# Attention and state space in one kernel: a smaller table base built on GpSimd, value sums dealt period by period, and a reordered tail

## The chip, the cores and the metric

The kernel runs on one core of a Trainium2 chip. The metric is the device time of one launch in microseconds; a figure quoted for a kernel is the median of its runs (at a granted clock of 0.995 to 1.0). The profile's span is some 1.8 us shorter than the device time of the same run (920.3 for 922.11), so spans are compared with spans and times with times.

## The reference, cut to what matters

Two layers read the same input x (2048 tokens, 1024 features, bf16), and a gate mixes them.

```python
g = sigmoid((x * gate_w).sum(-1, keepdims=True))
# a: state space, 1024 complex states, a scan over 2048 tokens
h_t = Lam_bar * h_{t-1} + (x @ B_bar.T)_t
a   = 2.0 * einsum("blp,dp->bld", h, Cmat).real + x * Dskip
# b: attention, 32 heads of 32 features
q, k, v = split(x @ wqkv)
b = softmax(q @ k.T * 32 ** -0.5) @ v   ... @ wo
return g * a + (1 - g) * b
```

The softmax has 32 x 2048 x 2048 = 134 million exps. They set the scale of everything that follows.

## The kernel before

The attention is cut into 512 **bursts**. A burst is 4 heads x 256 keys x 256 queries: 8 score matmuls fill two slots of PSUM, the memory that matmuls write to (two banks each), and ScalarE takes the exp of each slot (128x1024). A **half burst** is one of which VectorE computes half of the first exp by integer arithmetic; ScalarE then does 128x512 and 128x1024. `DVB` is the list of them.

```python
def exp(self, B, z, s):
    ...
    if z == 0 and B in DVB:
        self.dve_exp(B, s, p)          # ScalarE 128x512, VectorE the other 512 in four steps
    else:
        self.act(lambda e: e.activation(self.tile[p], ps[:, 2 * s:2 * s + 2, :], ACT.Exp, ...), [("S", s)], [("pt", p)], "exp")
```

From score to score of the next burst is one **period**. In it TensorE does the burst's 8 score matmuls, some **quarters** (a quarter is a fourth of an earlier burst's value sums: 4 matmuls of 128x33) and some **wide** matmuls (128x512) of whatever else the kernel needs: projections, the state-space products, the output product. (The value projection's are 128x128; four of them count as a wide one here.) The wide ones come in chains of 8 or 16 (a few of 7), all of them into the one PSUM bank 7, and after a chain VectorE has to copy that bank out before the next chain may start.

```python
for p in range(first, NBURST):
    second = self.burst(p)                    # 8 score matmuls, first exp
    head, tail = self.split_pv(p, ntail)      # this period's quarters: most ahead of, a few behind the wide ones
    self.pv(head)
    second()                                  # second exp
    quota = 3 if p in DVB else 5 if p + 1 in DVB and ... else MM_PER_PERIOD     # 4
    while used < quota:                       # wide matmuls; chains all go to bank 7
        ...
    self.pv(tail)
    ...
    ended.evac()                              # VectorE empties bank 7 after a chain's end
```

How many quarters a period takes is decided ahead, by a simple rule, in `plan`: five, or three in a half burst and in the period ahead of one (now and then one more).

```python
cap = 5
if p in DVB or p + 1 in DVB:
    cap = 3
```

The exps of a burst lie in a ring of tiles until their quarters have run, so quarters can't be put off for long.

## Time and profile before

| | before |
|---|---|
| device time, median of 6 runs | 921.74 us (921.26 to 922.04) |
| span of the profiled run | 920.3 us |
| TensorE / ScalarE / VectorE / GpSimd busy | 884.9 / 904.4 / 758.0 / 6.5 us |
| start to first exp | 9.8 us |
| first exp's start to last exp's end | 901.7 us |
| last exp's end to the span's end | 8.8 us |

Two engines are near 100%, and the question is which of them sets the end and how much is lost between. The prediction below shows the lines and reads them. The costliest groups of the page before: line, engine, operation, output and inputs, shapes, count, then busy time and mean ns, then idle time before them and what ended it. PE is TensorE, PEld its weight loads, ACT ScalarE, DVE VectorE, POOL GpSimd, SP the engine whose sequencer issues most DMAs; a q behind a name means the sequencer.

### The profile page before, as it was taken

To read this page: it belongs to the slowest core of one execution; us is meant where nothing else is said; L and a number is where in the kernel's file an instruction comes from. 1 tells how busy PE (TensorE), PEld (TensorE's weight loads), DVE (VectorE), ACT (ScalarE), POOL (GpSimd) and SP (SyncE) were. 2 spreads that over 40 slices of the span, in tenths; PEclk is the share of its full clock that TensorE was granted. 3 is DMA by queue.
4 is the path that set the end of the run, shared out by engine and by line. 5 is a ranking of instruction groups with operands and counts; after the bars stand their busy time and mean duration, and the time that the engine had idled before them with its cause. 6 is when DMAs were issued, how large, how long until landed. Compare 5 with 4: busy or idle time off the path is not lost.

```text
span 920.3 us, 33392 instructions
## 1 busy us (share of the span) xinstructions
PE 884.9 (96%) x14969; PEld 516.3 (56%) x15188; DVE 758.0 (82%) x1369; ACT 904.4 (98%) x1034; POOL 6.5 (1%) x31
## 2 busy tenths in 40 slices
PE   8999999999999999999999999999999999999996
PEld 4556655755575555565557555556655655555553
DVE  2799999999989889999889975669999866675665
ACT  6999999999999999999999999999999999999996
POOL 0000000000000000000000000000000000000000
PEclk9999999999999999999999999999999999999998
DMA  9546822213302324112142113123320212524312
GB/s 200 111 82 114 120 48 40 47 42 73 82 9 56 62 59 93 47 36 53 51 82 43 42 46 86 44 63 53 51 64 8 68 60 82 162 78 131 113 63 75
DMA packets 166436, 65.35 MB, mean 71 GB/s; under 512 B 146704, under 2 KB 154896, under 8 KB 166288
## 3 DMA queue, kind: packets, MB, share of 16 engines
q1 hardware_dynamic: 164128, 62.62, 30.6%
q8 instruction: 120, 1.97, 0.9%
q10 hardware_dynamic: 2160, 0.53, 0.3%
q14 instruction: 28, 0.23, 0.1%
HBM read 21.24 MB, written 12.58 MB: 37 GB/s over the span
## 4 chain that ended last, share of the span: by engine, by line
ACT 69%; PE 25%; DVE 2%; SPq 1%; issue 1%; DMA 1%; DVEq 0%
ACT f_pt L1693 59%; PE f_ps L1765 7%; PE f_ps L1677 5%; PE f_ps L1513 4%; PE f_ps L1485 4%; PE f_ps L1453 3%; ACT f_wb L1716 2%; ACT f_OT L1693 2%; ACT f_Et L1693 2%; ACT f_cT_re L1693 2%; ACT f_cT_im L1693 2%; PE f_ps L1473 1%; ACT f_ub L1716 1%; SPq L1080 1%; DMA f_xT<-in_A_x_dram 1%
## 5 line engine op out<-in xcount | busy, mean ns | idle before, releaser
L1693 ACT ACTIVATE f_pt<-f_ps 128x1024 bf16<-128x1024 f32 x848 | 801.8, 1141 | 1.2 <-PE f_ps L1677 1.0
L1765 PEld LDWEIGHTS f_ps<-f_V,f_pt 128*128 128x128 bf16 x6784 | 235.0, 96 | 136.5 <-issue 86.6
L1765 PE MATMUL f_ps<-f_V,f_pt 128*128 128x33 bf16 x6784 | 288.4, 178 | 0.3
L1677 PE MATMUL f_ps<-f_Q,f_K 32*128 32x256 bf16 x4096 | 217.9, 273 | 6.8 <-ACT f_cT_re L1693 1.0
L1677 PEld LDWEIGHTS f_ps<-f_Q,f_K 32*128 32x128 bf16 x4096 | 70.3, 92 | 122.6 <-ACT f_pt L1693 62.3
L1485 PE MATMUL f_ps<-f_xT,f_wb 128*128 128x512 bf16 x449 | 117.5, 377 | 7.2 <-issue 2.4
L1453 PE MATMUL f_ps<-f_xT,f_wb 128*128 128x512 bf16 x406 | 106.6, 378 | 5.0 <-issue 1.0
L1399 DVE TENSOR_TENSOR_SCAN f_ht<-f_pf,f_init,f_ut 128x512 bf16<-128x512 f32 x64 | 81.0, 1274 | 0.0
L1717 DVE TENSOR_SCALAR f_wb<-f_ps 128x512 f32<-128x512 f32 x77 | 52.8, 686 | 27.7 <-PE f_ps L1677 27.2
L1513 PE MATMUL f_ps<-f_cT_im,f_hp 128*128 128x512 bf16 x183 | 69.1, 378 | 3.0 <-DVE f_Ag L1522 0.5
L1540 PE MATMUL f_ps<-f_wb,f_OT 128*128 128x512 bf16 x219 | 58.0, 378 | 2.1 <-DVE f_xT L1546 0.2
L1473 PE MATMUL f_ps<-f_wb,f_xT 128*128 128x128 bf16 x896 | 59.1, 219 | 0.0
L1485 PEld LDWEIGHTS f_ps<-f_xT,f_wb 128*128 128x128 bf16 x512 | 40.2, 96 | 33.4 <-issue 1.2
L1513 PE MATMUL f_ps<-f_cT_re,f_hp 128*128 128x512 bf16 x153 | 57.8, 378 | 0.6
L1716 ACT ACTIVATE f_wb<-f_ps 128x512 bf16<-128x512 f32 x77 | 53.8, 699 | 0.0
L1724 DVE SCALAR_TENSOR_TENSOR f_wb<-f_Ag,f_wb 128x512 int16<-128x512 f32 x77 | 52.7, 684 | 0.7
L1723 DVE SCALAR_TENSOR_TENSOR f_Ag<-f_wb,f_Ag 128x512 f32<-128x512 uint16 x77 | 52.7, 685 | 0.6
L1722 DVE SCALAR_TENSOR_TENSOR f_Ag<-f_wb 128x512 f32<-128x512 uint16 x77 | 52.6, 683 | 0.1
L1453 PEld LDWEIGHTS f_ps<-f_xT,f_wb 128*128 128x128 bf16 x464 | 36.2, 96 | 28.7 <-issue 0.4
L1473 PEld LDWEIGHTS f_ps<-f_wb,f_xT 128*128 128x128 bf16 x896 | 50.5, 97 | 0.2
L1546 DVE SCALAR_TENSOR_TENSOR f_xT<-f_ps,f_gcol,f_hp 128x512 bf16<-128x512 f32 (+1 forms) x28 | 21.0, 751 | 26.6 <-PE f_ps L1540 26.6
L1391 DVE TENSOR_TENSOR f_tq<-f_ht,f_Et 128x1024 bf16<-128x1024 bf16 x64 | 42.5, 685 | 0.3
(143 smaller groups left out, 872.1 us busy)
## 6 DMA issues: line engine op xcount, KB each, us to landing
ag_scratch<-f_Ag SPq DMA_DIRECT2D x32, 256.0 KB, 2.0
f_hp<-ag_scratch SPq DMA_DIRECT2D x32, 256.0 KB, 2.8
f_wb<-in_B_wqkv_dram SPq DMA_DIRECT2D x21, 256.0 KB, 4.1
out_dram<-f_xT SPq DMA_DIRECT2D x16, 256.0 KB, 2.0
f_xa<-in_A_x_dram SPq DMA_DIRECT2D x32, 64.0 KB, 2.0
f_pf<-in_A_x_dram SPq DMA_DIRECT2D x32, 64.0 KB, 2.0
f_wb<-in_B_wo_dram SPq DMA_DIRECT2D x1, 1024.0 KB
f_OT<-f_On SPq DMA_TRANSPOSE x63, 2.3
```

The lines of the kernel that those rows point to most:

```text
L1399: ops.append((1.192, lambda ri=ri: dve(lambda e: e.tensor_tensor_scan(ht[:, ri, :], rr, ut[:, ri, :], self.init[:, ri, j:j + 1], ALU.mult, ...
L1453: mms.append((1, lambda e, f, l, a=a: e.matmul(ps[:, bank, :], w[:, g % 2, part, a, :], xT[:, a, 512 * ch:512 * (ch + 1)], start=f, stop=l ...
L1473: m = e.matmul(ps[:, bank, 128 * q:128 * (q + 1)], xT[:, a, 128 * kt:128 * (kt + 1)], w[:, g % 2, 2, a, :], start=(a == 0), stop=(a == 7))
L1485: mms.append((1, lambda e, f, l, a=a: e.matmul(ps[:, 7, :], bT[:, n % 2, ri, a, :], xT[:, a, 512 * ch:512 * (ch + 1)], start=f, stop=l), [ ...
L1513: mms.append((1, lambda e, f, l, j=j, ri=ri: e.matmul(ps[:, 7, :], hp(tq, ri, j), cT[ri][:, j, 512 * cb:512 * (cb + 1)], start=f, stop=l), ...
L1540: mms.append((1, lambda e, f, l, j=j: e.matmul(ps[:, 7, :], OT[:, j, 256 * qb + 128 * r:256 * qb + 128 * (r + 1)], wo[j][0][:, 512 * cb:51 ...
L1677: m = e.matmul(ps[:, 2 * sl[z] + h % 2, 256 * kl:256 * (kl + 1)], K[32 * h:32 * h + 32, g % 2, 128 * kt:128 * (kt + 1)], Q[32 * h:32 * h + ...
L1693: self.act(lambda e: e.activation(self.tile[p], ps[:, 2 * s:2 * s + 2, :], ACT.Exp, bias=OCTAVES * LN2, scale=LN2 / 128), [("S", s)], [("p ...
L1716: self.S.op("act", lambda e: e.activation(t[:, 0, :], ps[:, 2 * s, :], ACT.Exp, bias=OCTAVES * LN2, scale=LN2 / 128), reads=[("S", s)], wr ...
L1717: self.S.op("dve", lambda e: e.tensor_scalar(xi, ps[:, 2 * s + 1, :], BITS_0, BITS_MIN, ALU.add, ALU.max), reads=[("S", s)], writes=[("xi" ...
L1723: (0.603, lambda: self.dve(lambda e: e.scalar_tensor_tensor(xw, lo, CUBE_C, xw, ALU.add, ALU.mult), [I, W], [W], "exp_c")),
L1765: m = e.matmul(ps[:, 6, o:o + 33], self.tile[p][:, h2, 256 * kl + 128 * qt:256 * kl + 128 * (qt + 1)], V[:, g % 2, 2 * i + kl, h, :], star ...
```

## The change

The intent was to take work from ScalarE and VectorE and to even out TensorE's periods:

- The table of powers that the scan needs was built on VectorE from products of 512. Now GpSimd makes a base of 128 steps (six operations), and VectorE doubles it twice.
- From burst 72 on the quarters of a period are chosen as the kernel is built: as many as fit under the estimated end of ScalarE's exps, at most 7, never fewer than the tile ring forces (`least`).
- The lists `ORDER` (which chain comes when) and `DVB` (half bursts: 96 before, 102 after, none past burst 506) are new.
- The last burst's exps are split by query rows instead of heads, so that one row half can be normalized while the other is in ScalarE. The output is stored in four parts instead of two, and the long range check runs before the tail.
- The last four partial output products are prepared in two parts, and the second part is issued three times over (the result of the last counts).

The diff has 776 lines; this is its core, with cuts marked.

```diff
-DVB_RUNS = ((65, 65), (70, 70), ... (501, 501), (508, 508))
+DVB_RUNS = ((70, 70), (73, 73), ... (493, 497), (502, 506))
+PV_FREE = 72
+PV_MOST = 7
+PV_ROUND = 0.5
...
+    def pv_pick(self, p, dense, ta):
+        todo = self.pv_todo[self.pv_done // 32]
+        ready = sum(1 for t in todo if t[0] <= p)
+        least = self.pv_need[p] - self.pv_done
+        n = int((ta - self.T - QK_PE - dense * MM_PE - 0.1) / PV_PE + PV_ROUND)
+        n = max(min(n, PV_MOST), least, 1)
...
+        for n, (u, v) in enumerate(((0, 0), (1, 1), (0, 1), (1, 0))):
+            self.pool(lambda e, n=n, u=u, v=v: e.tensor_tensor(pr[n], hi[u], lo[v], ALU.mult), ...)
+            if n % 2:
+                self.pool(lambda e, ...: e.tensor_tensor(out, pr[n - 1], pr[n], ALU.add if r else ALU.subtract), ...)
...
+        if kind == "rest":
+            def again(e, f, l):
+                for _ in range(3):
+                    m = e.matmul(ps[:, 7, :], OT[:, 7, ...], wo[7][0][:, ...], start=True, stop=True)
+                return m
...
+        if B == NBURST - 1:
+            for t in range(2):
+                self.act(lambda e, t=t: e.activation(<row half t of all four heads>, ACT.Exp, ...), [("S", 1), ("S", 2)], ...)
```

## The prediction

> **What bounds the kernel now.** I read the page first: the busy line of the engines, the chain that ended last, and the top group.
>
> ```profile
> span 920.3 us, 33392 instructions
> ...
> PE 884.9 (96%) x14969; PEld 516.3 (56%) x15188; DVE 758.0 (82%) x1369; ACT 904.4 (98%) x1034; POOL 6.5 (1%) x31
> ...
> ACT 69%; PE 25%; DVE 2%; SPq 1%; issue 1%; DMA 1%; DVEq 0%
> ...
> L1693 ACT ACTIVATE f_pt<-f_ps 128x1024 bf16<-128x1024 f32 x848 | 801.8, 1141 | 1.2 <-PE f_ps L1677 1.0
> ```
>
> ScalarE (ACT) is busy 98% and holds 69% of the chain. It does nothing but softmax exps: 512 bursts of scores, two exps of 128x1024 each. In 96 bursts VectorE takes half of the first exp, so that ScalarE does 928 full exps (848+24+20+18+18 in the groups by shape) and 96 half ones (77+19). But PE is at 96%, so "busy" hides small losses. They show only in the distance from start to start. The second view is the timeline of ACT in the opening (start, length, engine, line, tile):
>
> ```profile
> 23.10 1.05 ACT L1693 ACTIVATE f_cT_re<-f_ps 128x1024 bf16<-128x1024 f32 x1
> 24.01 1.07 ACT L1693 ACTIVATE f_cT_im<-f_ps 128x1024 bf16<-128x1024 f32 x1
> 24.91 1.08 ACT L1693 ACTIVATE f_cT_re<-f_ps 128x1024 bf16<-128x1024 f32 x1
> ```
>
> The spans are 1.05 us or more and overlap; a new exp starts every 0.904 us (23.10, 24.01, 24.91). Taken over all starts in the trace, the least distance is 0.904 us after a full exp (its median too) and 0.477 us after a half one. So ScalarE's **floor** is 928 x 0.904 + 96 x 0.477 = 838.9 + 45.8 = 884.7 us. The first exp starts at 9.82, the last ends at 911.52: 901.7 us, so some 17 us are lost between exps. What stays is 9.8 us of opening and 8.8 us of tail.
>
> Third, where those 17 us go. Summing the distance over the floor, burst by burst: bursts 16 to 71 lose 2.7 us, 72 to 500 lose 13.2 us, 501 to 510 0.2 us; the rest is opening. Nearly every large loss comes before a burst's first exp and waits for its scores (PE, L1677). An example from the timeline of 644.7 to 649:
>
> ```profile
> 644.76 0.51 PE L1677 MATMUL f_ps<-f_Q,f_K 32*128 32x256 bf16 x8
> 645.20 0.47 PE L1765 MATMUL f_ps<-f_V,f_pt 128*128 128x33 bf16 x12
> 645.52 1.24 PE L1485 MATMUL f_ps<-f_xT,f_wb 128*128 128x512 bf16 x5
> 646.59 0.36 PE L1765 MATMUL f_ps<-f_V,f_pt 128*128 128x33 bf16 x8
> 646.88 0.40 PE L1677 MATMUL f_ps<-f_Q,f_K 32*128 32x256 bf16 x8
> ```
>
> One period: 8 score matmuls, 20 value-sum matmuls (5 quarters of 4), 5 wide ones. Scores come again after 2.12 us, while two full exps need 1.81 us. The kernel's own constants (scores 0.34, a quarter 0.101, a wide matmul 0.2157, 0.1 over) give 0.34+0.505+1.079+0.1 = 2.02 us here, and 1.91 for 6 quarters and 4 wide, where the trace has 1.905. I sorted the 429 periods from 72 to 500 by that formula. In 39 PE is over ScalarE's floor by more than 20 ns: **5.2 us** lost. In 35 it is not, yet over 60 ns are lost (**5.3 us**), mostly where a wide chain waits for VectorE to empty its bank. The others add 2.7 us of crumbs. In sum PE needs 690 us there by the formula and ScalarE 736: the work fits, it is badly dealt.
>
> Fourth, the end of the chain of waits, in order of time:
>
> ```profile
> 912.03 0.17 DVE f_rc L2060
> ...
> 912.23 0.37 DVE f_On L2063 x2
> ...
> 913.24 0.61 PE f_ps L2078 x2
> 913.84 0.11 PE f_ps L2081
> ...
> 914.05 0.68 DVE f_xT L2091
> 914.73 0.34 DVEq L2149
> 915.07 0.24 DVE f_xT L2091
> ```
>
> This serial tail follows the last exp (ends 911.52): reciprocal, normalize, transpose, output product, addition. The sequencer records add that the last store is issued at 915.39 to 915.72, and its sixteen parts land from 917.31 to 919.81; instruction-fetch packets of 8 and 16 KB run among them from 915.7 on. Then 0.45 us to the end.
>
> **What the Trainium skill says.** "ScalarE: Activation LUTs", on what ACT_TABLE_LOAD costs, gives 280 ns + 0.833 ns per element for an ACTIVATE with a pointer bias, 1133 ns at 1024, and an overlap of some 93 ns back to back. The lengths agree (1106 median), the overlap does not: starts are 904 ns apart, and I use that. "GPSIMD Engine Reference", 3.1, has a tensor_tensor of 2048 fp32 elements at 4497 ns, twice VectorE's; no run here has a large one yet (the largest in the trace is 128x8, 0.2 to 0.3 us). "Runtime: NRT & Kernel Launch", Instruction fetch mechanics, says a taken branch outside the current pages forces a fetch by DMA; the packets at the end of this trace agree.
>
> **The change part by part.**
> Exps: the two lists of bursts count 96 and 102. Six more halves move to VectorE: 6 x (0.904 - 0.477) = **-2.6 us** of ScalarE's floor. The last burst's exps by row halves keep their size.
>
> VectorE: six more exps cost 6 x 4 x 0.685 = 16.4 us. The tables cost 16 x 1.215 + 16 x 0.685 = 30.4 us before; after, by the costs written in the change, 8 x 2.35 = 18.8, so -11.6. The sine chain goes from 400 to 224 columns: 19 instructions at about 0.47 to 0.34, some -2.5. The 24 small copies at 0.161 go to GpSimd: -3.9. Sum -18: VectorE comes out level. GpSimd gets 6 operations of 1024 elements, an estimate from the skill's figure of 2.25 us each, 13.5 us in a row. They can start once the sine chain is done, which the new spare slots put near 26 us; ready near 40, just when the tables are wanted (the opening's 16 bursts end at 38.6). I count 0.
>
> Value sums dealt per period: from burst 72 on, a period takes as many quarters as fit under ScalarE's end, at most 7. With 5 wide matmuls it takes 3 instead of 5, with 4 it takes 5, with 3 it takes 7. The 39 overfull periods go, but rounding and the limits of the tile ring leave some: 5.2 to about 1, **-4.2 us**. Of the 5.3 us of late banks little: **-0.8 us**. Before burst 72 nothing.
>
> Tail: one query row half is finished while the other's exp runs, so one normalize (0.27) leaves the path, the flag product (0.11) goes behind, the reciprocal is cheaper. Against it, on VectorE the short check (0.8 us) and two additions (2 x 0.68) stay in a row after the last normalize. From the last exp's end E: value sums to E+0.42, reciprocal and normalize to 1.05, check to 1.85, additions to 3.25, last store issued by E+3.65, where it was E+4.2: -0.55. The stores are four of half the size, two queues are used, and the branches come after the last issue rather than before, so that fewer packets should stand behind fetches: another -1 of the 2.5 us between first and last landing. Together **-1.5 us**. The repeated product in the last four partial outputs adds 8 wide matmuls on PE, 1.7 us, where PE has 2.9 us spare over ten periods: 0.
>
> Sum: -2.6 - 5.0 - 1.5 = -9.1; 921.7 - 9.1 = **912.6 us**.
>
> **Rivals.**
> PE as the bound: it is 96% busy and a full period with 5 quarters and 4 wide ones takes 1.81 us by the formula, all that ScalarE gives. If shorter exps only turn into waits for scores, the -2.6 goes and half of the dealing: 917. For it: those balanced periods lose 35 ns on average already. Against: 46 us of slack over 429 periods.
> VectorE and GpSimd: if the base is late, VectorE stands in order before its table work, the bank is not emptied, and ScalarE stalls in the opening; likewise six more exps among slices where DVE already shows 9. For it: 13.5 us in a row on GpSimd is only an estimate. Worth +2 to +4: 915 to 917.
> The dealing works better than I grant: all overfull periods and half of the late banks vanish, crumbs halve: -4 more, 908.
> The end: fetches still hit the stores; then -0.5 for -1.5, 913.6.
>
> **Range and chances.** The middle is 912.6; rivals push up 1 to 5 and down 4. I take 907.5 to 917.5. Over 2% faster means below 903.3, that is 9.8 + 882.1 + a 7 us tail with almost no loss: 0.03. Slower by 2%: 0.01.
>
> **What would show it.** ScalarE's groups: 922 exps of 128x1024 and 102 of 128x512. The loss between exps at 11 to 13 us instead of 17; no period with 5 wide matmuls and 5 quarters past burst 72. On GpSimd six operations near 2.2 us ending by 41 us, and no long wait of VectorE for POOL. From the last exp's end to the span's end 7.3 us instead of 8.8. The prediction is wrong if periods with 4 wide matmuls lose more than before, or if VectorE waits for GpSimd.

## More of the kernel before

```profile
L1485 PE MATMUL f_ps<-f_xT,f_wb 128*128 128x512 bf16 x449 | 117.5, 377 | 7.2 <-issue 2.4
...
L1485 PEld LDWEIGHTS f_ps<-f_xT,f_wb 128*128 128x128 bf16 x512 | 40.2, 96 | 33.4 <-issue 1.2
```

Every matmul of this line loads its weights once. So 512 were run and the trace has the records of 449.

## The result, and the profile after

| | before | after |
|---|---|---|
| device time, median of 6 runs each | 921.74 us | 918.81 us (918.65 to 919.24) |
| ratio of fast runs, 95% interval | | 0.9969 (0.9956 to 0.9982) |

Ratios here are the mean time of one kernel's fast runs over that of the other's in the same rounds, so not quite the ratio of the medians. The change won 2.9 us where 9.1 were predicted, and 918.8 lies above the range of 907.5 to 917.5. The result is correct.

The page after, its busy line, its chain that ended last and the top groups of ScalarE:

```profile
span 916.8 us, 33709 instructions
...
PE 902.4 (98%) x15196; PEld 513.6 (56%) x15196; DVE 757.3 (83%) x1394; ACT 902.1 (98%) x1034; POOL 33.4 (4%) x63
...
PE 92%; DVE 3%; ACT 3%; DMA 1%; issue 0%; SPq 0%
...
L1781 ACT ACTIVATE f_pt<-f_ps 128x1024 bf16<-128x1024 f32 x840 | 800.5, 1156 | 1.2 <-PE f_ps L1758 0.6
```

VectorE is level, as foreseen. But the chain seems to have gone from ScalarE (69%) to TensorE (92%), and TensorE's busy time rose by 17.5 us, though the change adds only 1.7 us of matmuls. That is a trap. This time no record is missing:

```profile
L1517 PE MATMUL f_ps<-f_xT,f_wb 128*128 128x512 bf16 x512 | 131.1, 377 | 1.5 <-DVE f_ub L1523 0.4
...
L1517 PEld LDWEIGHTS f_ps<-f_xT,f_wb 128*128 128x128 bf16 x512 | 40.3, 96 | 34.2 <-issue 2.2
```

The changed kernel was run once more later (after_control below), and that trace again lacked 219 records. The same kernel then reads like this:

```profile
PE 882.0 (96%) x14977; PEld 513.5 (56%) x15196; DVE 757.4 (83%) x1394; ACT 902.3 (98%) x1034; POOL 33.4 (4%) x63
...
PE 75%; ACT 18%; DVE 3%; issue 2%; SPq 1%; DMA 1%
```

Seven of the twenty traces lack 217 to 219 records, the one of before among them. evac_less_before below, which has the matmuls of before and lacks no record, shows PE busy for 903.5 us and in 71% of the chain. So neither PE's busy time nor the chain's shares may be compared between a full trace and one with gaps. What is safe are the exps, of which each trace has all 1024, and LDWEIGHTS, which agree with the program in all traces.

From the exps' starts, the span falls into these stages (us; the third column is the repeat of after):

| stage | before | after | repeat |
|---|---|---|---|
| to the first exp | 9.82 | 9.77 | 9.66 |
| bursts 0 to 15 | 29.68 | 29.40 | 29.68 |
| bursts 16 to 71 | 103.06 | 103.08 | 103.07 |
| bursts 72 to 500 | 749.54 | 747.86 | 747.45 |
| bursts 501 to 510 | 17.39 | 17.42 | 17.42 |
| burst 511, to the last exp's end | 2.03 | 2.05 | 2.05 |
| tail | 8.79 | 7.26 | 7.26 |

Two stages moved: bursts 72 to 500 by -1.7 (-2.1 in the repeat), the tail by -1.5. (The profiled run of before, 922.11 us, is 0.4 over its median, so the stages differ by more in sum than the medians do.) In 72 to 500 the **floor** of ScalarE (0.904 us for each full exp, 0.477 for each half one, as in the prediction) fell from 736.3 to 733.4, by 3.0, since there are 7 more half bursts in that stage. But the loss over the floor rose from 13.2 to 14.5 us, where I had it fall by 5.0. Sorted by the kind of period (matmuls counted by their weight loads; rare kinds left out):

| periods of 72 to 500 | before: number, mean loss | after: number, mean loss |
|---|---|---|
| full, 5 quarters, 5 wide | 38, 127 ns | none |
| full, 4 quarters, 5 wide | none | 23, 109 ns |
| full, 3 quarters, 5 wide | 46, 44 ns | 57, 46 ns |
| full, 5 quarters, 4 wide | 139, 24 ns | 153, 9 ns |
| full, 6 quarters, 4 wide | 6, 71 ns | 5, 68 ns |
| all full bursts | 337, 11.4 us in sum | 330, 8.6 us in sum |
| half, 3 quarters, 3 wide | 81, 12 ns | 72, 45 ns |
| half, 4 quarters, 3 wide | none | 14, 73 ns |
| half, 5 quarters, 3 wide | none | 6, 203 ns |
| all half bursts | 92, 1.8 us in sum | 99, 5.9 us in sum |

The dealing helped in the full bursts (-2.8 us), most of all in those with four wide matmuls, and gave more than that back in the half ones (+4.1). The 5.9 us of the half bursts have two parts: 2.2 are lost after the 20 with four or five quarters; and of the 72 with three quarters, the 28 in whose period TensorE stands over 60 ns at a chain's start lose 2.7, the other 44 only 0.5. An example of each from the timeline of the kernel after (start, length, engine, line, tiles). The first is a half burst with five quarters (20 value matmuls, of which the cut lines leave 8 to see):

```profile
841.00 0.40 PE L1758 MATMUL f_ps<-f_Q,f_K 32*128 32x256 bf16 x8
...
841.32 0.37 PE L1853 MATMUL f_ps<-f_V,f_pt 128*128 128x33 bf16 x8
841.43 0.64 ACT L1804 ACTIVATE f_ub<-f_ps 128x512 bf16<-128x512 f32 x1
...
841.74 0.81 PE L1578 MATMUL f_ps<-f_wb,f_OT 128*128 128x512 bf16 x3
841.92 1.06 ACT L1781 ACTIVATE f_pt<-f_ps 128x1024 bf16<-128x1024 f32 x1
...
842.58 0.29 PE L1758 MATMUL f_ps<-f_Q,f_K 32*128 32x256 bf16 x4
```

From scores to scores TensorE takes 842.58 - 841.00 = 1.58 us without a gap, and ScalarE has 0.477 + 0.904 = 1.38 us of work: 0.2 us are lost. The second is a half burst in which a chain starts:

```profile
703.72 0.40 PE L1758 MATMUL f_ps<-f_Q,f_K 32*128 32x256 bf16 x8
703.83 0.69 DVE L1493 CAST f_K<-f_ps 128x512 bf16<-128x512 f32 x1 [0.20 <-PE f_ps L1485]
...
704.05 0.47 PE L1853 MATMUL f_ps<-f_V,f_pt 128*128 128x33 bf16 x12
...
704.66 0.83 PE L1505 MATMUL f_ps<-f_wb,f_xT 128*128 128x128 bf16 x12
```

VectorE empties bank 7 until 703.83 + 0.69 = 704.52. The three quarters, issued at some 25 ns a matmul, are through by 704.05 + 12 x 0.025 = 704.35. The next chain starts at 704.66: 0.3 us of TensorE are lost, and the period takes 1.70 us for a floor of 1.38.

GpSimd did what was foreseen, and VectorE found the base ready (the timeline of POOL; the first table operation of VectorE comes at 40.13):

```profile
26.24 3.82 POOL L1319 TENSOR_TENSOR f_hp<-f_rc 128x1024 f32<-128x1024 f32 x2 [23.33 <-DVE f_rc L1310]
...
36.36 2.36 POOL L1323 TENSOR_TENSOR f_OT<-f_hp 128x1024 f32<-128x1024 f32 x1
```

The tail after, from the chain of waits in order of time (start, length, what; the last exp ends at 909.58):

```profile
910.06 0.21 PE f_ps L2173 x8
...
910.51 0.37 DVE f_On L2181 x2
...
913.48 0.69 DVE f_xT L2203
```

### The profile page after: what moved, and what is told of

Same layout as the page of the kernel before. It is cut to its first block, busy times and chain, and to the rows that moved or that the text cites. A ratio compares the mean times of both kernels' runs of the same rounds, so it can differ in the third digit from the quotient of the medians.

```text
span 916.8 us, 33709 instructions
## 1 busy us (share of the span) xinstructions
PE 902.4 (98%) x15196; PEld 513.6 (56%) x15196; DVE 757.3 (83%) x1394; ACT 902.1 (98%) x1034; POOL 33.4 (4%) x63
## 4 chain that ended last, share of the span: by engine, by line
PE 92%; DVE 3%; ACT 3%; DMA 1%; issue 0%; SPq 0%
PE f_ps L1853 26%; PE f_ps L1758 18%; PE f_ps L1545 12%; PE f_ps L1517 12%; PE f_ps L1485 11%; PE f_ps L1578 6%; PE f_ps L1505 5%; ACT f_cT_re L1781 1%; DVE f_tq L1423 1%; ACT f_pt L1781 1%; DMA f_xT<-in_A_x_dram 1%; ACT f_cT_im L1781 1%; ACT f_Et L1781 1%; ACT f_OT L1781 1%; DVE f_ht L1431 1%
## 5 line engine op out<-in xcount | busy, mean ns | idle before, releaser
L1758 PE MATMUL f_ps<-f_Q,f_K 32*128 32x256 bf16 x4096 | 213.1, 273 | 2.6 <-ACT f_cT_re L1781 1.2
L1517 PE MATMUL f_ps<-f_xT,f_wb 128*128 128x512 bf16 x512 | 131.1, 377 | 1.5 <-DVE f_ub L1523 0.4
L1485 PE MATMUL f_ps<-f_xT,f_wb 128*128 128x512 bf16 x464 | 119.0, 378 | 0.3 <-DVE f_Q L1490 0.2
L1805 DVE TENSOR_SCALAR f_wb<-f_ps 128x512 f32<-128x512 f32 x83 | 56.8, 685 | 27.4 <-PE f_ps L1758 26.5
L1545 PE MATMUL f_ps<-f_cT_re,f_hp 128*128 128x512 bf16 x192 | 72.6, 378 | 0.9 <-DVE f_Ag L1554 0.8
L1578 PE MATMUL f_ps<-f_wb,f_OT 128*128 128x512 bf16 x248 | 63.9, 378 | 0.2
L1804 ACT ACTIVATE f_wb<-f_ps 128x512 bf16<-128x512 f32 x83 | 60.8, 732 | 0.6 <-PE f_ps L1758 0.6
L1812 DVE SCALAR_TENSOR_TENSOR f_wb<-f_Ag,f_wb 128x512 int16<-128x512 f32 x83 | 56.7, 683 | 0.6
L1811 DVE SCALAR_TENSOR_TENSOR f_Ag<-f_wb,f_Ag 128x512 f32<-128x512 uint16 x83 | 56.7, 683 | 0.5
L1810 DVE SCALAR_TENSOR_TENSOR f_Ag<-f_wb 128x512 f32<-128x512 uint16 x83 | 56.6, 682 | 0.3
L1523 DVE CAST f_ub<-f_ps 128x512 bf16<-128x512 f32 x48 | 33.1, 690 | 14.8 <-PE f_ps L1517 14.1
```

Of the source, the lines that this page charges most:

```text
L1485: mms.append((1, lambda e, f, l, a=a: e.matmul(ps[:, bank, :], w[:, g % 2, part, a, :], xT[:, a, 512 * ch:512 * (ch + 1)], start=f, stop=l ...
L1517: mms.append((1, lambda e, f, l, a=a: e.matmul(ps[:, 7, :], bT[:, n % 2, ri, a, :], xT[:, a, 512 * ch:512 * (ch + 1)], start=f, stop=l), [ ...
L1545: mms.append((1, lambda e, f, l, j=j, ri=ri: e.matmul(ps[:, 7, :], hp(tq, ri, j), cT[ri][:, j, 512 * cb:512 * (cb + 1)], start=f, stop=l), ...
L1578: mms.append((1, lambda e, f, l, j=j: e.matmul(ps[:, 7, :], OT[:, j, 256 * qb + 128 * r:256 * qb + 128 * (r + 1)], wo[j][0][:, 512 * cb:51 ...
L1758: m = e.matmul(ps[:, 2 * sl[z] + h % 2, 256 * kl:256 * (kl + 1)], K[32 * h:32 * h + 32, g % 2, 128 * kt:128 * (kt + 1)], Q[32 * h:32 * h + ...
L1804: self.S.op("act", lambda e: e.activation(t[:, 0, :], ps[:, 2 * s, :], ACT.Exp, bias=OCTAVES * LN2, scale=LN2 / 128), reads=[("S", s)], wr ...
```

## The experiments

Runs of the kernel before on the same chip (medians 921.64, 921.28, 921.58, 922.15, 921.58). **My theory** after the traces: TensorE and ScalarE need nearly the same time in almost every period, neither has slack to lend from one period to the next, and the new dealing pushes quarters into half bursts and away from the boundaries between chains. **Rival A**: ScalarE alone is the bound and the loss is latency. **Rival B**: TensorE alone is the bound, as the chain's 92% suggest. **Rival C**: VectorE is too full to empty the bank in time.

### Which engine is the bound: 42 us less of TensorE, 29 us less of ScalarE, both

pe_less cuts one matmul of eight in each chain from 512 to 32 columns, act_less the full exps from burst 100 on from 1024 to 976 elements. pe_less is wrong; act_less leaves some exps stale and yet stays in tolerance. My texts put pe_less at 30 us. The traces have 218 shortened matmuls, after which the next one starts 25 ns later and not 215, or the next scores 110 and not 311: about 42 us. For act_less, 727 exps (in after) that may follow 0.04 us sooner are the 29 us expected.

```diff
-  mms.append((1, lambda ...: e.matmul(ps[:, bank, :], w[...], xT[:, a, 512 * ch:512 * (ch + 1)], ...)))
+  n = 32 if a == 3 else 512          # the same in the u, c and output chains
+  mms.append((1, lambda ...: e.matmul(ps[:, bank, 0:n], w[...], xT[:, a, 512 * ch:512 * ch + n], ...)))
```

```diff
-  e.activation(self.tile[p], ps[:, 2 * s:2 * s + 2, :], ACT.Exp, ...)
+  n = 488 if B >= 100 else 512
+  e.activation(self.tile[p][:, :, 0:n], ps[:, 2 * s:2 * s + 2, 0:n], ACT.Exp, ...)
```

> The kernel before, with one wide matmul in each chain of eight (two in each of sixteen) cut from 512 to 32 columns: about 200 matmuls, some 30 us of TensorE work less, everything else as it was; the result is wrong on purpose. Theory 1 (TensorE's work is as long as ScalarE's, its seeming slack of 46 us was lost matmul records): the 13 us lost between the exps fall to about 4, so 912 us. Theory 2 (the prediction's own: ScalarE alone is the bound, TensorE only badly dealt): the overfull periods go, 915 to 917 us. Theory 3 (banks emptied late by VectorE): 919 or more.

> The kernel before, with every full exp from burst 100 on cut from 1024 to 976 elements: some 730 exps by 0.04 us, 29 us of ScalarE work less; the result is wrong on purpose. Theory 1: TensorE takes over at once, no more than 5 us are won, 917 us or more. Theory 2: with 46 us of slack on TensorE most of it is won, 895 to 902 us. Theory 3: most of it too, the late banks stay, 897 to 905 us.

> The kernel after with the same cut of TensorE work. Theory 1: from 918.8 to some 909 us, a larger fall than before, as ScalarE's floor is 2.6 us lower and the six halves become visible. Theory 2: 916 us. Theory 3: 917 us or more.

> The kernel after with the same cut of ScalarE work. Theory 1: 914 us or more. Theory 2: 892 to 900 us. Theory 3: 894 to 902 us.

> The kernel after with both cuts of the last runs: TensorE by some 30 us and ScalarE by 29. Each alone won only 4. Theory 1b (the two are equally long period by period, and what one spares in one period cannot be kept for the next): the two cuts together win more than the sum of both, 15 us or more: 904 us or less. Theory 3 (late banks rule): the sum at most, 911 us or more. The result is wrong on purpose.

| run | time, us | ratio to before (95%) | against its own base |
|---|---|---|---|
| pe_less_before | 918.98 | 0.9975 (0.9959 to 0.9992) | -2.7 |
| act_less_before | 917.94 | 0.9960 (0.9943 to 0.9977) | -3.7 |
| pe_less_after | 914.60 | 0.9924 (0.9907 to 0.9941) | -4.2 |
| act_less_after | 914.93 | 0.9928 (0.9911 to 0.9944) | -3.9 |
| both_less_after | 893.62 | 0.9699 (0.9682 to 0.9715) | -25.2 |

(The base is the kernel before, 921.64, or the first figure of after, 918.81.) In pe_less_after the pauses among the eight score matmuls of a burst, summed over bursts 72 to 500, grew from 50 to 88 us: TensorE waits there for about as long as it no longer works. The chains that ended last say who is left as the bound; pe_less_after:

```profile
ACT 90%; PE 8%; SPq 1%; DMA 1%; DVE 0%; issue 0%
```

and act_less_after:

```profile
PE 90%; DVE 4%; ACT 3%; DMA 1%; issue 1%; SPq 0%; DVEq 0%
```

**What follows.** Either cut alone wins 3 to 4 us, both together 25: more than three times the sum. That refutes rivals A and B: both engines are the bound. That they are so period by period shows in the trace of pe_less_after. In bursts 72 to 500 it still loses 11.1 us over ScalarE's floor, where after loses 14.5. The 191 periods that hold a shortened matmul lose 2.0 us instead of 6.9; the 238 that hold none lose 9.1 instead of 7.6. What TensorE saves in one period does not help in another. (Only 10 of the 99 half bursts hold a shortened matmul.) It also shows what the 46 us of my prediction were worth: with some 40 us of real slack in that stage (3 and the 191 shortened matmuls) the kernel after takes 914.6; I had predicted 912.6 from a slack that wasn't there.

### The late bank: shorter evictions, and a less busy VectorE

evac_less copies 128 instead of 512 columns out of bank 7 after most chains (wrong); that takes 49 us off VectorE's busy time (757.3 to 708.3). dve_less leaves the evictions alone and cuts 48 of the 64 scans from 512 to 192 columns, 30 us of VectorE. (My text miscounts the scans; its 30 us are what the trace shows, 757.3 to 727.0.)

```diff
-  self.dve(lambda e: e.tensor_copy(self.ub[k][:, ri, :], ps[:, 7, :]), ...)
+  m = 128 if ch else 512             # the same for q, k, v from the fourth group on, and c
+  self.dve(lambda e: e.tensor_copy(self.ub[k][:, ri, 0:m], ps[:, 7, 0:m]), ...)
```

```diff
-  dve(lambda e: e.tensor_tensor_scan(ht[:, ri, :], rr, ut[:, ri, :], ...))
+  m = 512 if ch == 0 else 192
+  dve(lambda e: e.tensor_tensor_scan(ht[:, ri, 0:m], rr[:, 0:m], ut[:, ri, 0:m], ...))
```

> The kernel after, with the instructions by which VectorE empties the wide chains' bank cut from 512 to 128 columns (u and c chains and the projections from group 3 on), so that the bank is free some 0.4 us sooner; TensorE and ScalarE work unchanged, the result wrong on purpose. Theory 3b (dealing filled the light periods in which the waits for the bank hid): TensorE's waits for the bank, 11.6 us from burst 72 to 500, nearly go, and 4 to 6 us are won: 913 to 915 us. Theory 1b alone: under 2 us, 917 us or more.

> The kernel before with the same cut. Theory 3b: there the waits for the bank were partly hidden in light periods, so less is won than after: 1.5 to 3.5 us, 918 to 920 us. Theory 1b alone: under 2 us, 920 us or more.

> The kernel after, with the 112 scans on VectorE that come after the first chunk cut to between a third and a half of their length (16 of 128 stay): about 30 us of VectorE work less, the instructions that empty the bank unchanged, the result wrong on purpose. If banks are late because VectorE is busy with something else when they are due, 2 to 4 us are won (915 to 917); if it is the time of emptying itself, under 1 us (918 or more).

| run | time, us | ratio to before (95%) | against its base | TensorE's stall at chain starts, 72 to 500 |
|---|---|---|---|---|
| evac_less_after | 915.32 | 0.9934 (0.9917 to 0.9951) | -3.5 | 11.6 to 2.4 us |
| evac_less_before | 920.04 | 0.9989 (0.9972 to 1.0005) | -1.2 (unclear) | 8.9 to 2.3 us |
| dve_less_after | 917.87 | 0.9970 (0.9951 to 0.9988) | -0.9 | |

**What follows.** The late bank costs some 3.5 us after and 1.2 before by the totals, 3.1 (747.7 to 744.64) and 2.0 (749.54 to 747.56) by the stage of bursts 72 to 500. So the change made it worse, by 1 to 2 us. The 30 us taken from VectorE elsewhere win 0.9 by the median (0.7 in the stage, nothing by the ratio, in which one run of 920.47 weighs), and leave 10.3 of the 11.6 us of stall. Even scaled up to 49 us that is less than half of what evac_less_after wins. So VectorE's load (rival C) is a small part at most; the main one is the length of the one copy between two chains. Why it got worse shows at the 183 boundaries between chains in that stage. With six or more quarters between a chain's end and the next one's start the mean stall is 5 ns in the kernel after; with five it is 92, with four 154, with three 219. Before, it was 28 ns with six or more, then 61, 116 and 149 (with the gaps of that trace filled in from the steady spacing, so roughly). Boundaries with three quarters went from 5 to 12, those with six or more from 96 to 88. So there are more short boundaries, and each costs more; why the same count costs more is not shown. In the code, the choice of a period's quarters looks at ScalarE's clock and not at the bank.

### The tail, undone

oldtail_after is the kernel after with the tail of the kernel before (one normalize for both row halves, exps by heads, long check in the tail, two stores); all before the last burst stays, but for the rotation of the score slots that the new tail needs.

```diff
-  sl = [(2 * self.p + 2) % 3, (2 * self.p + 3) % 3]
+  sl = [(2 * self.p) % 3, (2 * self.p + 1) % 3]
...
-  <tail of after>
+  <tail of before>
```

> The kernel after with the tail of the kernel before put back (one normalize for both row halves, last exps by heads, the long range check in the tail, two full-width stores); everything up to the last exp stays. My theory: the tail is worth what the two traces show between the last exp's end and the span's end, 8.8 us against 7.2, so this kernel takes +1.5 us: about 920.3. The rival: the 1.6 us are the luck of where instruction fetches fall among the last stores; then the tail's own serial part gives 0.5 us and the time is about 919.3.

It took 920.04 us (919.5 to 921.09), ratio 0.9982 (0.9969 to 0.9996), 1.2 us over after. Its profiled run was its slowest, and there bursts 0 to 15 took 30.37 us, which are 29.40 in most traces: a hitch of the opening of 0.8 to 1 us that some runs have and that has nothing to do with the tail. Its tail itself took 9.20 us against 7.26. In the traces with the tail of before and ScalarE's work unchanged (before, pe_less_before, evac_less_before, oldtail_after) the tail takes 8.56 to 9.20 us; in after and its repeat 7.26 both times. So the tail's step is real, and the rival's 0.5 falls; its size is open between the 1.2 us of the total and the 1.9 of this one trace.

### Dealing quarters earlier ahead of eight half bursts

Undoing the dealing as a whole is not possible: the lists of chains and half bursts are tuned to it, and the kernel before's rule, or a cap of four quarters in half bursts, does not build with them (quarters come too late for the tile ring). So I went the other way and mended it. In after, 20 of the half bursts hold 4 or 5 quarters, each time because the ring forced them. even_after takes them earlier ahead of eight such bursts. Quarters over three in half bursts fall from 26 to 15, by a count over the built program.

```diff
+EVEN = (301, 308, 329, 397, 473, 477, 493, 497)
...
+        soft = dict(need)
+        for p in range(NBURST - 1, PV_FREE, -1):
+            soft[p - 1] = max(soft[p - 1], soft[p] - (3 if p in EVEN else PV_MOST))
...
-        n = max(min(n, PV_MOST), least, 1)
+        n = max(min(n, PV_MOST), least, min(self.pv_soft[p] - self.pv_done, ready, PV_MOST), 1)
```

> The kernel after with one edit in the dealing: ahead of eight half bursts, quarters that the tile ring would force into them are dealt some periods earlier. Quarters over three in half bursts fall from 26 to 15. Theory (half bursts are overfull): by the kernel's own constants a fourth quarter makes a half period 73 ns too long and a fifth 204 ns, so 11 quarters less give -0.8 to -1.2 us: about 917.8; the loss between exps after half bursts falls from 5.9 to about 4.8. Rival (only the bank wait counts): the number of quarters between two wide chains hardly changes (154 missing to six before, 149 after), so 0: 918.7.

It took 917.79 us (917.68 to 918.22), ratio 0.9959 (0.9945 to 0.9973), correct. Bursts 72 to 500 take 747.01 us; four traces of kernels with after's order of work there (after, after_control, oldtail_after, again1_after) take 747.86, 747.45, 747.60 and 747.87, 747.7 in the mean. So -0.7 in the stage where it acts and -1.0 in the total. The loss after half bursts is 5.2 us instead of 5.9. The periods of half bursts with 4 and 5 quarters still lose 75 and 205 ns each; there are 7 and 4 of them instead of 14 and 6. A second kernel with this dealing, even_again1 below, has 747.15. Both lie below all four of after. The theory's size holds in the total, a little less in the stage; the rival's zero does not.

### Moving quarters to where the bank is late: a miss, and its repair

spread_after leaves the number of quarters in each period and changes, for 84 periods, how many of them run behind the wide matmuls, so that more lie between two chains. The table comes from a search over the built program. spread_even does this on top of even_after.

```diff
+TAIL = {21: 3, 27: 3, 33: 3, ... 451: 3}
...
+            ntail = TAIL.get(p, ntail)
             head, tail = self.split_pv(p, ntail)
```

> The kernel after with the same quarters in every period, but of 84 periods the number that run behind the wide matmuls instead of ahead is set by a table, so that between the end of one wide chain and the start of the next there are at least six quarters nearly everywhere. The missing quarters (to six, summed over all boundaries) fall from 154 to 41. Theory (the single bank of the wide chains is late because VectorE has not emptied it): the stall of PE before a new chain in bursts 72 to 500 falls from 11.6 us to about 4, and the time by 2.5 to 3.5 us, as it did with shorter evictions: 915.3 to 916.3. Rival (PE is full anyway and the stall only moves into waits for scores, or the quarters behind the wide matmuls delay the next scores): the stall falls, the time stays within 0.7 us of 918.8, or rises.

> Both edits together: quarters dealt earlier ahead of eight half bursts, and the table of quarters behind the wide matmuls, searched again for that dealing (missing quarters 154 to about 37). Theory: the two losses are different ones and add, 918.8 - 3.0 - 1.0 = about 914.8. Rival: both cure the same stalls, then it is no better than the better of the two, 915.8.

Both gave a **wrong** result (relative error 0.139), unintended. In a period that ends a unit of eight bursts the normalize follows the quarters ahead of the wide matmuls; the table moved quarters of such periods behind it. The times were 917.22 and 917.07, ratios 0.9955 (0.9941 to 0.9969) and 0.9951 (0.9938 to 0.9965), and the stall at chain starts was 6.4 and 5.5 us instead of 11.6. The two runs' errors agree in every digit, which speaks for a wrong order rather than a race. The repair leaves such periods alone, at the price of fewer boundaries mended.

```diff
-            ntail = TAIL.get(p, ntail)
+            if not ends:
+                ntail = TAIL.get(p, ntail)
```

> The table of quarters behind the wide matmuls, searched again and not applied in periods that end a unit (whose last quarters must run before the normalize; that was the mistake). Missing quarters between wide chains: 154 in after, 41 in the wrong version, 86 here, 60% of the way. Theory (late bank): the stall of PE before new chains falls from 11.6 us to about 8.5, and as the wrong version turned 5.2 us of stall into 1.6 of time, the time falls by about 1.0: 917.8, with a correct result. Rival (the wrong version won by its wrong order, since units closed earlier): no gain, 918.8.

> Both edits in valid order: the quarters dealt earlier ahead of eight half bursts, and the mended table (missing quarters 154 to 77). If the two losses are different ones they add: 918.8 - 1.0 - 1.0 = 916.8. If they are mostly the same stalls, as the wrong version suggests (917.22 with the table alone, 917.07 with both), it is 917.4 to 917.8. The result is to be correct.

| run | time, us | ratio to before (95%) | bursts 72 to 500, us | stall at chain starts, us |
|---|---|---|---|---|
| after (four traces) | 918.81 | 0.9969 (0.9956 to 0.9982) | 747.7 | 11.2 to 11.6 |
| even_after | 917.79 | 0.9959 (0.9945 to 0.9973) | 747.01 | 10.8 |
| spread_right | 917.80 | 0.9951 (0.9937 to 0.9965) | 747.12 | 8.5 |
| spread_even_right | 918.26 (916.91 to 918.34) | 0.9954 (0.9941 to 0.9968) | 746.31 | 7.3 |

All are correct. The median of spread_even_right misleads: its five runs are 916.91, 916.93, 918.26, 918.33 and 918.34, two groups 1.4 us apart. The profiled one is of the fast group, with 29.41 us for bursts 0 to 15; spread_right's profiled run had 30.17 there. That the slow group is the hitch of the opening is likely, but no trace of one of its runs is at hand. In the stage where the edits act the readings are clean: -0.7 for the dealing, -0.6 for the spreading, -1.4 for both. The two losses are different ones and add (all_mended below, with both, has 746.44). The spreading won something outside the stage too: its table also moves quarters of the last bursts, and the tail takes 6.90 us in spread_right and 6.89 in spread_even_right instead of 7.26. But 3.1 us less of stall bring only 0.6 us; most of a stall that is removed turns up as waiting elsewhere, as in pe_less.

### The repeated output product

again1_after issues the second part of the last four partial output products once instead of three times.

```diff
-                for _ in range(3):
+                for _ in range(1):
```

> The kernel after with the repeated product in the last partial outputs issued once instead of three times: 8 wide matmuls, 1.7 us of TensorE, are gone between bursts 501 and 510. The prediction counted them as free, since PE had 2.9 us spare there: then the time stays at 918.8, within 0.3. Rival: TensorE is co-bound there as elsewhere and they cost up to their own length: 917.1.

It took 918.15 us (917.79 to 920.29), ratio 0.9962 (0.9948 to 0.9976), correct. Here the trace says more than the total. The last exp ends at 909.59 us against 909.58, so nothing changed between the exps, as I had counted. But the tail takes 6.46 us instead of 7.26. In the timeline of TensorE in the kernel after, three of these products stand right ahead of the last value sums:

```profile
907.77 0.82 PE L1574 MATMUL f_ps<-f_wb,f_OT 128*128 128x512 bf16 x3 [0.19 <-DVE f_xT L1584]
908.43 0.76 PE L1853 MATMUL f_ps<-f_V,f_pt 128*128 128x33 bf16 x24
909.04 1.02 PE L2162 MATMUL f_ps<-f_Et,f_ident 128*128 128x512 bf16 x4
909.90 0.36 PE L2173 MATMUL f_ps<-f_V,f_pt 128*128 128x33 bf16 x8
```

and in again1_after only one. The tail's first value sums (L2173, of the first row half) now start 0.78 us earlier, at 909.12 while the last exp still runs, as the new tail was meant to do:

```profile
907.43 0.38 PE L1574 MATMUL f_ps<-f_wb,f_OT 128*128 128x512 bf16 x1
907.65 0.76 PE L1853 MATMUL f_ps<-f_V,f_pt 128*128 128x33 bf16 x24
908.25 1.02 PE L2162 MATMUL f_ps<-f_Et,f_ident 128*128 128x512 bf16 x4
909.12 0.36 PE L2173 MATMUL f_ps<-f_V,f_pt 128*128 128x33 bf16 x8
```

My "0" for these matmuls was wrong by 0.8 us. The 2.9 us of spare time that it rests on were 2.0 when counted by weight loads, which the 1.7 us still fit over ten periods; in the last period they did not.

### The cures together, beside the changed kernel itself

after_control is the changed kernel unaltered; even_again1 is even_after with the product issued once; all_mended is spread_even_right with the product issued once.

> The changed kernel itself, on the same chip as the two below, as their measure: 918.8 within 0.5.

> Quarters dealt earlier ahead of eight half bursts, and the repeated output product issued once. The first acts between bursts 300 and 500, the second on the last 2 us of TensorE before the tail (the tail went from 7.3 to 6.5 us in again1_after), so they should add: 918.8 - 1.0 - 0.7 = 917.1. Rival: the last exps would end earlier anyway and something else of the tail binds: 917.8.

> The three cures together: quarters dealt earlier, the mended table of quarters behind the wide matmuls, the output product once. spread_even_right took 916.9 in its undisturbed runs (a stage of the opening that sometimes takes 0.8 to 1 us longer made 918.3 of others), even_after 917.7: with the tail's 0.7 it makes 916.2. Rival: late banks and overfull half bursts are mostly the same stalls, then it equals even_again1, 917.0.

| run | time, us | ratio to before (95%) | bursts 72 to 500, us | tail, us |
|---|---|---|---|---|
| after_control | 918.39 (918.00 to 918.56) | 0.9962 (0.9949 to 0.9976) | 747.45 | 7.26 |
| even_again1 | 917.38 (917.12 to 917.70) | 0.9952 (0.9938 to 0.9965) | 747.15 | 6.47 |
| all_mended | 916.90 (916.55 to 917.90) | 0.9951 (0.9937 to 0.9964) | 746.44 | 6.52 |

All are correct, and the control came out within the 0.5 that I gave it. On one chip all_mended is 1.5 us ahead of after by the medians and 4.7 ahead of before, and thus the fastest of the kernels here that do all the work. I had expected 916.2 of it and 917.1 of even_again1; by the medians both won less. In the stages the cures do add: 747.45 - 746.44 = 1.0 and 7.26 - 6.52 = 0.7, together 1.7 of the 1.8 us between the two spans (916.6 and 914.8). The intervals of the ratios of after_control and all_mended overlap, since each is taken against before; it is the stages that carry the verdict.

## Why the prediction was right or wrong

- **ScalarE's floor, -2.6: right.** In bursts 72 to 500 it fell by 3.0 (seven more half bursts there, one fewer before), and the groups have 922 exps of 128x1024 and 102 of 128x512 in all.
- **VectorE level, GpSimd in time, 0: right.** VectorE is busy 757.3 us instead of 758.0. Two products take 3.82 us and an addition 2.36, where I had 2.25 for each; the base is ready at 38.72, and no wait of VectorE for GpSimd is in the trace. Two small readings of mine were off: burst 16 starts at 39.5 and not 38.6, and two of GpSimd's 128x8 operations took 0.6 to 0.7 us, not 0.2 to 0.3.
- **Value sums dealt per period, -5.0: this is the step that failed**, with the sentence under it, "In sum PE needs 690 us there by the formula and ScalarE 736: the work fits, it is badly dealt", and the "46 us of slack over 429 periods" that set aside the rival of PE as the bound. The loss between exps in that stage rose by 1.3 us. The miss of 6.3 us is the whole of the prediction's error; floor, opening and tail make up the rest within 0.4.
 - The 690 us were counted from matmul records, and the trace before lacks 189 wide ones between bursts 72 and 500 (against their LDWEIGHTS). At 0.2157 us each these are 40.8 us. Counted by LDWEIGHTS, TensorE needs 730.6 us and ScalarE 736.3: the slack was under 6 us, and after the change 3. The sorting had the same fault: overfull were 49 periods with 6.1 us of loss, not 39 with 5.2, and the late ones 26 with 4.4, not 35 with 5.3. The page's own busy line, with x14969 matmuls and x15188 weight loads, would have warned me.
 - Even true slack would not have helped as I used it, as pe_less_after shows, which has some 40 us of it in that stage and still loses 11.1. A light period can't pay for a heavy one: the scores of the next burst need a slot that an exp has to leave first, so TensorE is never far ahead. From a burst's fourth score, the last that its first exp needs, to that exp it is 0.33 us at least and 0.46 to 0.48 in the mean, before and after. Summed period by period, TensorE is over ScalarE's floor by 11.3 us before and 7.8 after, and that part did fall. That it does not show is due to the next point.
 - Late banks, "-0.8": they got worse instead, by 1 to 2 us as the two evac_less runs have it. And half bursts, which I left out of the sum because they lost hardly anything before, took the quarters that the ring forces: 20 of them have 4 or 5. They lost 4.1 us more; even_after shows that undoing 11 of the 26 quarters brings back 0.7 to 1.0.
- **The test that I named for it pointed at the wrong periods.** I wrote that periods with 4 wide matmuls would lose more. The full ones lose less (24 to 9 ns for the commonest); the half ones with 3 wide are what went wrong. The other sign, no period with five of each past burst 72, came true, but 23 periods with four quarters and five wide took their place and lose 2.5 us. The sum of the loss, the first of my tests, did show it. From the first exp to the last one's end there are 909.58 - 9.77 = 899.8 us, and the floor is 922 x 0.904 + 102 x 0.477 = 882.1: 17.7 us where I had 11 to 13.
- **Tail, -1.5: the sum right by luck, its terms wrong.** I had 7.3 us and the trace has 7.26. But the last store is issued 5.0 us after the last exp's end and not 3.65: before it was 4.2. The queue's timeline has it (start, length until the third store is issued; the exp ends at 909.58):

```profile
913.29 1.30 SPq L2208 DMA_DIRECT2D out_dram<-f_xT  x3
```

From there to the end are 2.25 us, where before there were 4.6. So the serial part grew by 0.8 instead of shrinking by 0.55, and the landing shrank by 2.3 instead of 1. The 0.8 are the repeated products, shown by again1_after (last store 4.2 us after the exp, tail 6.46). Without them the serial part is as long as before, so the predicted -0.55 did not come from the new shape either. The parts of the last store before landed from 917.31 to 919.81, among packets of instruction fetch; after, those of all four stores from 914.83 to 916.26, ahead of most fetches (from 916.19 on). That it is the fetches' place that matters is argued from the traces, not shown by an experiment of its own.
- **The rival that came true** is "PE as the bound", with the 917 that I gave it (918.8 measured; 918.4 in the repeat). I saw the balanced periods and the 35 ns that they lose (24 when counted by weight loads), and let a sum over a stage overrule them.

What stays open: how the 6.7 us that the kernel after loses over its period-by-period sum (14.5 against 7.8) split among the bank, the waits of scores for slots and crumbs. No edit takes one of them away alone, as removed stall partly moves. Nor does any run separate the new lists `ORDER` and `DVB` from the dealing: the -2.6 of the six half bursts is arithmetic on the floor.

## What to carry to other kernels

Before you call one of two nearly full engines slack, count its work from records that you have checked against another kind (weight loads against matmuls, calls against the program), and sum the excess period by period: slack helps only as far as the buffers let one engine run ahead of the other. A scheduler that levels one resource will fill exactly those light places in which another wait had been hidden, here the copy of a single PSUM bank; give it that wait as a constraint. And work that is free on the average of ten periods may not be in the last one, where nothing follows to hide it.

## What the Trainium skill lacked or had wrong

- "Perfetto Trace Analysis", Tensor Engine Instruction (MATMUL, LD_WEIGHTS), says that ends of matmuls are estimated, but not that records can be missing: here 219 of 15188 (before) and 219 of 15196 (the repeat of after), none in the first trace of after. The chain's share of TensorE for the same kernel was 92% and 75%.
- "TensorE: Matmul & The Clock Gate", Back-to-back issue gap, gives 131 ns per matmul of 512 columns sustained in a stream of weight loads and matmuls, and calls its formula's 216 too high. Here the median step between two wide matmuls is 0.215 us and the least 0.214 (1136 steps, bursts 72 to 500 of after), which is the 215.7 ns that another section of the page has as measured.
- "ScalarE: Activation LUTs", What ACT_TABLE_LOAD costs, has an overlap of about 93 ns back to back. Exps of 128x1024 with a length of some 1106 ns start 904 ns apart, an overlap of some 200 ns.
- "GPSIMD Engine Reference", 3.1, has one figure for tensor_tensor, an addition of 2048 fp32 elements at 4497 ns. Halved for 128x1024, an estimate, it makes 2.25 us; measured were 1.91 for a product whose two inputs are broadcast and 2.36 for an addition of two plain ones.
- No page that I read says how far a store's landing varies with its place at the end of a program: the last store took 4.6 us from its issue to the span's end before and 2.25 after.
- No page speaks of an opening that now and then takes 0.8 to 1 us longer (bursts 0 to 15: 29.4 us in most traces, 30.17 and 30.37 in two).
